# Attention and two mixture layers in one kernel: whole-unit loads of queries, keys and values, and the first weight pair in three tiles of 256 columns

## The chip, the core and the metric

The kernel runs on one core of one Trainium2 chip. The metric is the device time of one execution in microseconds (us), as a median over runs. The engines are named as the profile names them: PE (TensorE matmul) and PEld (its weight loads), DVE (VectorE), ACT (ScalarE), POOL (GpSimd) and SP (SyncE, which issues all DMAs here).

## What is computed

The reference chains three stages; the input sizes stand in the comments.

```
# q, k, v: (2, 8, 768, 64); mem_k, mem_v: (2, 8, 8, 64)
for c in range(24):                       # chunks of 32 queries
    k_full = concat([mem_k, k[:, :, c*32-16 : c*32+32+8]])      # v_full alike
    scores = q_c @ k_full^T / sqrt(64);  a = softmax(scores)
    out[:, :, chunk c] = a @ v_full
x = out as (1536, 512)                    # 2 x 768 tokens, 8 heads x 64
for e in range(4):                        # p: rows of domain_probs, normalised
    y += p[:, e:e+1] * (relu(x @ w1[e]) @ w2[e])                # 512 -> 1024 -> 512
h = y @ w_in;  g = max(h, 0) + alpha * min(h, 0)                # 512 -> 2048
return g @ w_out                                                # 2048 -> 512
```

## The kernel before

**Matmuls.** All large products run in two-part float32r: each operand is split into a high part (`xh`, `wh`) and a low part (`xl`, `wl`), and three matmuls (high by high, high by low, low by high) make one product. The activations are stored transposed: 512 features as four blocks of 128 partitions, the 1,536 tokens as two halves of `NCOL` = 768 columns. The first matmul of every layer (`gemm1`) is a Strassen-like scheme of seven products named a, b, c, d on the PSUM banks they use: 7 x 6 = 42 matmuls a tile. The second (`gemm2`) has 48 matmuls a tile, into `y`. A "pair" `p` is a block of 2 x 128 hidden features; there are 16 pairs of the first layer (`NP1`) and 8 of the second. A "tile" is a pair and a range of columns: `FIRST` lists the ranges for pair 0, all other pairs have two tiles of 384 columns. From pair 1 on the order is gemm1 of the next tile, then gemm2 of this one. For pair 0 all tiles but the last run gemm1 and gemm2 one after the other, which the code calls `tight`.

**Attention.** A unit `u` (0 to 11) is 128 queries of all eight heads. Its work in PE's order is: scores (`two`, 32 matmul instructions, which the trace shows as 64), four transposes (`t`), values (`x`, shown as 32), four transposes back (`xt`). Between them DVE takes the maximum (`mx`) and subtracts it (`pe`), ACT takes the exponential, DVE divides (`dn`, `rd`, `xs`), and ACT, DVE and POOL turn the result into `acc`, `xh` and `xl`, the operands of gemm1, with the sums and differences that the scheme needs (`st`). An even and an odd unit make 128 columns of both halves; c = u // 2 numbers them.

**Order.** `att_cycle` runs the units before the first tile, one a cycle, with some dummy matmuls (`keep`) in each. When enough units are through (`att["five"]`, checked per tile as `c0 + n` over 128), the tile begins, and the remaining units are started by `att_poll` between its matmuls, one each `PACE` of a planned clock `now`. Instructions of each engine stay in the order in which the code emits them; DMAs that are issued through `nc.sync` instead of `sync` (`load`, `load_pb`) may be placed earlier by the scheduler. SP issues its DMAs one by one, and a DMA that waits holds up all behind it.

**Weights.** `prep_w1` and `prep_w2` load a pair's weights (`raw`), form the sums (`s`), and split them (`wh`, `wl`) on ACT and POOL. `gate` normalises the probabilities, `load_pb` spreads them over the partitions, and `convert` reads the second layer's weights, which are 64-bit (`fr`).

**Loads of attention.** Queries and keys of a unit come as two halves (four heads each) of 128 x 624 numbers, into `RING` = 8 buffers. Values come in four DMAs of 64 x 520 numbers, into `RING_V` = 5 half-unit buffers that are cleared once at the start. `load_next_half` and `load_v` issue the later loads from inside `unit`; a load waits until PE has read its buffer's former content.

Of the kernel before, what the change touches and what calls it, by code (L numbers as in the profile page):

```python
# [10 lines left out]
F32 = mybir.dt.float32  # L11
F32R = mybir.dt.float32r
# [6 lines left out]
B, H, S, D = 2, 8, 768, 64  # L19
# [3 lines left out]
NW = BLK // WIN  # L23
# [5 lines left out]
NU = B * NBLK  # L29
NT, DM = B * S, H * D  # L30
E, F1, F2 = 4, 1024, 2048
P = 128
KD = DM // P
HH = H // 2
HP = HH // 2
VW = 2 * HP * NW * (D + 1)
# [30 lines left out]
def tile_kernel(ctx: ExitStack, tc: tile.TileContext, qk, v, wa, wq, dpt, alpha, out):  # L67
# [125 lines left out]
    def mm(*a, n, took=None, **kw):  # L193
        pe_.matmul(*a, **kw)
        now[0] += took or 0.013 + n / 2.4e3


    qk_t = [bp.tile([P, QW + KW], F32, tag="gg" + "BA"[i // 4], bufs=4, name=f"qk{i}") for i in range(RING)]
    v_t = [bp.tile([P, V_ROOM], F32, name=f"v{i}", **tag)[:, :VW].rearrange("p (e z w d) -> p e z w d", e=2, z=HP, w=NW)
           for i, tag in enumerate((dict(tag="w2", bufs=4), dict(tag="w2", bufs=4), dict(tag="fr"), *2 * [dict(tag="v", bufs=2)]))]  # L200
    for vt in v_t:
        for e in range(2):
            (pool, dve)[e].memset(vt[:, e], 0.0)
# [2 lines left out]
    xs = xs.rearrange("p (z e d) -> p z e d", e=2, d=D)  # L206
    pe = pe.rearrange("p (z k e) -> p z k e", e=2, k=KEYS)

    def v_of(hu):
        return v_t[hu % RING_V]  # L210

    def qk_of(hu):
        return qk_t[hu % RING if hu < 2 * RING else hu % (RING // 2)]

    def load_half(hu):
        sync.dma_start(qk_of(hu), qk[hu // 2, :, hu % 2])

    def load_next_half(hu):
        if hu < RING:
            load_half(hu + RING)  # L220
        elif hu < RING + RING // 2:
            load_half(hu + RING)
        elif hu >= 2 * RING and hu + RING // 2 < 2 * NU:
            load_half(hu + RING // 2)

    v_next = [0]

    def load_v(hu):
        assert hu == v_next[0]
        v_next[0] += 1  # L230
        if hu >= 2 * NU:
            return
        for e in range(2):
            sync.dma_start(v_of(hu)[e::2, e].rearrange("p z w d -> p (z w d)"), v[hu // 2, e, :, hu % 2])

    def unit(u):

# [4 lines left out]
        s_ps = two[:, :, :2 * HP * KEYS].rearrange("p e (z k) -> p e z k", k=KEYS)  # L242
        now[0] += T_SW
        for half in range(2):
            qk_ = qk_of(2 * u + half)
            qv = qk_[:, :QW].rearrange("p (z q) -> p z q", q=BLK)
            kv = qk_[:, QW:].rearrange("p (z k) -> p z k", k=SPAN)
            for z in range(HP):
                for w in range(NW):
                    for e in range(2):  # L250
                        rows = slice(e * D, (e + 1) * D)
                        mm(s_ps[win[w], e, HP * half + z], qv[rows, z, win[w]], kv[rows, z, w * STEP:w * STEP + KEYS],
                           n=KEYS, took=T_S, start=True, stop=True)
            load_next_half(2 * u + half)
        mx = cp.tile([P, 2, 2 * HP], F32, tag="mx", bufs=2, name=f"mx{u}")
        dve.tensor_reduce(out=mx, in_=s_ps, axis=AX.X, op=ALU.max)
        dve.tensor_tensor(
# [15 lines left out]
        for z in range(2 * HP):  # L273
            half, i = divmod(z, HP)
            if z in CUT:
                n = CUT[z]
                parts.append((z, n, bank(f"x{u}_{z}")[:, :2 * n * (D + 1)].rearrange("p (z e d) -> p z e d", e=2, d=D + 1)))
            z0, _, x_ps = parts[-1]
            for w in range(NW):
                mm(x_ps[win[w], z - z0], pt[:, z, win[w]], v_of(2 * u + half)[:, :, i, w], n=2 * (D + 1), took=T_X,  # L280
                   start=True, stop=True)
            if i == HP - 1:
                load_v(2 * u + half + RING_V)
        dn = cp.tile([P, 2 * HP, 2, 1], F32, tag="dn", bufs=2, name=f"dn{u}")
        for z, n, x_ps in parts:
            dve.tensor_scalar_add(dn[:, z:z + n], x_ps[:, :, :, D:D + 1], 1e-9)
# [219 lines left out]
    def prep_w2(p):  # L506

        e, dt = pace(p in QUICK and p < NP1, p)
        if p in (NP1, NP1 + 1):
            dt = DT_NEAR  # L510
        yield pause(0.0, lambda: p < 2 or p - 2 in used2)
        if p == 1:
            yield pause(0.0, lambda: att["done"] == NU and (1, 1) in raws)
        if p:
            yield pause(max(0.0, landed[p, 1] - now[0]))
        if p == 0:
            yield pause(0.0, lambda: (0, 1) in raws and landed[0, 1] <= now[0] + 1.0)
        raw = raws[p, 1]
        h = bp.tile([P, 4, 256], F32R, tag="w2", bufs=4, name=f"wh2_{p}")
        l = bp.tile([P, 4, 256], F32R, tag="w2", bufs=4, name=f"wl2_{p}")  # L520
        for z in (0, 2):
            act.copy(h[:, z:z + 2], raw[:, z:z + 2])
            yield pause(1.5 * dt)
            e.tensor_tensor(
                out=l[:, z:z + 2], in0=raw[:, z:z + 2], in1=h[:, z:z + 2].bitcast(F32), op=ALU.subtract
            )
            if z == 2:
                w2[p] = (h, l)
                raws.pop((p, 1))
            yield pause(1.5 * dt)  # L530
        if p == NP1:
            load_raw(p + 2, 0)
        elif 0 < p < NP - 1:
            load_raw(p + 1, 1)
# [95 lines left out]
    def load_pb(e, c0, n, ab=(0, 1)):  # L630
        assert gated
        if (e, c0, n) not in pb_t:
            pb_t[e, c0, n] = bp.tile([P, 2, 384], F32, tag="pb", bufs=2, name=f"pb{e}_{c0}")
        sl = slice(ab[0], ab[-1] + 1)
        nc.sync.dma_start(pb_t[e, c0, n][:, sl, :n], p_dram[e, sl, c0:c0 + n].partition_broadcast(P))
# [20 lines left out]
    def gemm1(p, c0, n, parity, last):  # L656
# [29 lines left out]
        def gelu(blk, src):  # L686

            i, ab = divmod(blk, 2)

            lag_poll(lambda: len(glist) < 2 or glist[-2][1] in glist[-2][0])  # L690
            glist.append((gs, blk))
            if p >= NP1 and i == 0:
                if ab == 0:
                    g2 = bp.tile([P, 2, 384], F32, tag="pb", bufs=2, name=f"g2_{nm}")
                    gs["g2"] = g2
                g = gs["g2"][:, ab, :n]
            else:
                g = bp.tile([P, 384], F32, tag="g", bufs=4, name=f"g{blk}_{nm}")[:, :n]
            gg = bp.tile([P, 2, 384], F32R, tag="gg" + "AB"[parity], bufs=4, name=f"gg{blk}_{nm}")
            gh, gl = gg[:, 0, :n], gg[:, 1, :n]  # L700

            def high():
                act.copy(gh, g)
                pool.tensor_tensor(out=gl, in0=g, in1=gh.bitcast(F32), op=ALU.subtract)
                gs[blk] = (gh, gl)

            def whole():
                dve.scalar_tensor_tensor(out=g, in0=src, scalar=0.0, in1=g,
                                         op0=ALU.max, op1=ALU.add)
                later(0.8, high)  # L710

            if p < NP1:
                pb = pb_t[2 * p * P // F1, c0, n]
                dve.scalar_tensor_tensor(out=g, in0=src, scalar=0.0, in1=pb[:, ab, :n],
                                         op0=ALU.max, op1=ALU.mult)
                later(0.7, high)
            else:
                fi = 2 * (p - NP1) + i

                def negative():  # L720
                    act.activation(g, src, AF.Relu, scale=-1.0)
                    act.mul(g, g, nalpha[:, fi:fi + 1])
                    later(1.4, whole)

                later(0.0, negative)
# [141 lines left out]
        order += [(1, k), (2, k - 1)]  # L867
    order += [(2, len(tiles) - 1)]

    for kind, hu in (*[(load_half, i) for i in range(4)], (load_v, 0), (load_v, 1), (load_half, 4), (load_half, 5),  # L870
                     (load_v, 2), (load_v, 3), (load_half, 6), (load_half, 7), (load_v, 4)):
        kind(hu)
    stream("w", weights())
    streams["w"][0] = PREP0
    acts = {}
    begun = [
        *[(x, lambda: load_raw(0, 0, 4)) for x in (1, 1)],
        (2, lambda: sync.dma_start(praw, dpt.rearrange("e (p i) -> p e i", i=NI))),
        *[(x, lambda: load_raw(0, 0, 4)) for x in (2, 2)],
        (3, lambda: stream("g", gate())),  # L880
        (4, lambda: sync.dma_start(nalpha, alpha)),
        *[(x, lambda ab=ab: load_pb(0, *FIRST[0], (ab,))) for ab, x in enumerate((7, 7))],
        *[(x, lambda: load_raw(0, 1, 2)) for x in (8, 8)],
        (9, lambda: load_pb(0, *FIRST[1], (0,))),
        *[(x, lambda: load_raw(1, 0, 4)) for x in (9, 10, 10, 11)],
        (11, lambda: load_pb(0, *FIRST[1], (1,))),
        *[(x, lambda: load_raw(1, 1, 2)) for x in (12, 12)],
    ]

    def begin():  # L890
# [3 lines left out]
    for i, (what, k, *other) in enumerate(order):  # L894
# [3 lines left out]
        if what == 1:  # L898
# [18 lines left out]
                prep_force(f"x{c0}", lambda: f"x{c0}" not in streams)  # L917
            began.append(k)
            change[0] = kc - 1 <= k < kc + 8
            acts[k] = gemm1(p, c0, n, k % 2, k == final[p])  # L920
        else:
            change[0] = change[0] and k < kc + 6
            if other:
# [3 lines left out]
            if p == NP1 - 2:  # L927
                stream(f"x{c0}", transition(c0, n))

FIRST = [(0, 384), (384, 384)]  # L930
USE = (A11, S2, S1, A12, S3, S4, A22)
SLOTS = 10
WIDE = (NP1 - 1, NP1 + 1)
# [5 lines left out]
CUT = {0: 3, 3: 1}  # L939
FAST = (2, 5)  # L940
LIVE = 4
PACE = 3.8
PACE0 = 3.9
X_STEP = (0.8, 0.8, 0.0, 0.8, 0.8, 0.8)
PREP0 = 11.0

DT = 1.1
DT_0 = 0.78
# [4 lines left out]
DT_X = (1.1, 0.88)  # L953
X_WAIT = (0.0, 7.5)
DT_NEAR = 0.8
RING = 8
V_ROOM = 1152
RING_V = 5
WARM = 18
PAD = 16  # L960

# [73 lines left out]
```

## Time and profile before

| | |
|---|---|
| median of 3 runs | 819.87 us (819.07 to 821.52) |
| profiled execution | 818.88 us, of which the span of the trace is 817.1 us |
| PE busy | 799.2 us (98% of the span) |
| DVE, POOL, ACT busy | 582.5, 563.8, 330.8 us |
| DMA moved | 71.69 MB, of it 16.05 MB in the first 60 us |

PE's busy time is modelled from pipelined matmuls, so 98% says only that PE seldom stands still in what the trace can see; the time of a stretch follows from the starts of its matmuls. Shares are averages over two very different stages: attention, in the first 70 us, and the weight pairs after it.

### The profile page before, as it was taken

The page shows a single profiled execution, that of the slowest core. Times are in us where ns is not written, and L with a number is a line of the kernel's source. Part 1 is how long each engine was busy: PE and PEld are TensorE (multiplying, and loading weights), DVE is VectorE, ACT ScalarE, POOL GpSimd, SP SyncE. Part 2 cuts the span into 40 slices and gives each one's busy share as a digit, 9 for nine tenths or more (in the row PEclk, how much of TensorE's full clock was granted, in tenths as well). Part 3 has the DMA queues.
Part 4 walks back from the last instruction along what each step waited for, and adds up shares of the span by engine and source line. Part 5 has one row for each costly group of instructions (what it writes and reads, how often), then busy time and mean ns, then how long its engine had stood idle before and what let it go on. Part 6 is the DMA issues. An engine that isn't in the chain of part 4 may idle for free.

```text
span 817.1 us, 14814 instructions
## 1 busy us (share of the span) xinstructions
PE 799.2 (98%) x5623; PEld 785.3 (96%) x5623; DVE 582.5 (71%) x1116; ACT 330.8 (40%) x718; POOL 563.8 (69%) x587
## 2 busy tenths in 40 slices
PE   8789999999999999999999999999999999999998
PEld 6578999999999999999999999999899999999998
DVE  4687478777867768867777768587954877756555
ACT  3566523224133223232332323155572665456441
POOL 2777777777877877967887872293954987866611
PEclk9999999999999999999999999999999999999999
DMA  8882121331331431322432312001002142211004
GB/s 286 256 257 69 52 91 39 128 117 54 110 107 42 134 108 57 116 69 74 136 96 85 111 36 72 9 26 53 26 27 91 45 124 82 73 41 52 1 1 155
DMA packets 30503, 71.69 MB, mean 88 GB/s; under 512 B 4704, under 2 KB 9952, under 8 KB 30432
## 3 DMA queue, kind: packets, MB, share of 16 engines
q1 hardware_dynamic: 30432, 70.75, 26.5%
q8 instruction: 44, 0.72, 0.4%
q14 instruction: 27, 0.22, 0.1%
HBM read 59.18 MB, written 11.56 MB: 87 GB/s over the span
## 4 chain that ended last, share of the span: by engine, by line
PE 91%; DVE 3%; ACT 2%; POOL 2%; DMA 1%; issue 1%; DVEq 0%; ACTq 0%; POOLq 0%
PE y L61 48%; PE a L61 12%; PE c L61 11%; PE d L61 11%; PE b L61 6%; POOL gg L61 1%; PE two L61 1%; DMA qk<-in_qk 1%; DVE pe L61 1%; DVE mx L61 1%; PE x L61 1%; PE wps0.0_84 L61 0%; ACT pe L61 0%; DMA raw<-in_wa 0%; PE t L61 0%
## 5 line engine op out<-in xcount | busy, mean ns | idle before, releaser
L61 PE MATMUL y<-gg,wh 128*128 128x384 f32 x1540 | 397.6, 334 | 0.7 <-POOL gg L61 0.6
L61 POOL TENSOR_TENSOR gg<-g,gg 128x384 fp32r<-128x384 f32 x192 | 202.5, 1066 | 118.6 <-ACT gg L61 115.2
L61 PEld LDWEIGHTS y<-gg,wh 128*128 128x128 f32 x1540 | 278.2, 188 | 2.0 <-POOL gg L61 1.2
L61 PE MATMUL y<-gg,wl 128*128 128x384 f32 (+1 forms) x770 | 257.1, 334 | 0.0
L61 DVE TENSOR_TENSOR acc<-y,acc 128x384 f32<-128x384 f32 x321 | 172.1, 550 | 60.9 <-PE y L61 59.3
L61 ACT CAST gg<-g 128x384 fp32r<-128x384 f32 x192 | 97.6, 512 | 152.5 <-DVE g L61 152.3
L61 POOL TENSOR_TENSOR wl<-raw,wh 128x256 fp32r<-128x256 f32 (+1 forms) x112 | 114.3, 1030 | 50.1 <-ACT wh L61 36.2
L61 PEld LDWEIGHTS y<-gg,wl 128*128 128x128 f32 x770 | 144.5, 188 | 0.0
L61 ACT COPY u<-a 128x384 f32<-128x384 f32 x48 | 23.1, 481 | 195.2 <-PE a L61 195.2
L61 POOL TENSOR_TENSOR wl<-s,wh 128x256 fp32r<-128x256 f32 x88 | 68.2, 782 | 7.6 <-ACT wh L61 7.2
L61 DVE TENSOR_TENSOR u<-b,u 128x384 f32<-128x384 f32 x48 | 26.7, 557 | 61.2 <-PE b L61 57.6
L61 PE MATMUL d<-xh,wl 128*128 128x384 f32 x184 | 61.6, 335 | 0.0
L61 PE MATMUL d<-xh,wh 128*128 128x384 f32 x184 | 61.6, 335 | 0.0
L61 PE MATMUL d<-xl,wh 128*128 128x384 f32 x184 | 61.6, 335 | 0.0
L61 PE MATMUL a<-xh,wh 128*128 128x384 f32 x184 | 61.6, 335 | 0.0
L61 PE MATMUL a<-xl,wh 128*128 128x384 f32 x184 | 61.5, 334 | 0.0
L61 PE MATMUL a<-xh,wl 128*128 128x384 f32 x184 | 61.5, 334 | 0.0
L61 ACT CAST wh<-raw 128x256 fp32r<-128x256 f32 (+1 forms) x116 | 54.5, 492 | 15.4 <-PE y L61 14.8
L61 POOL TENSOR_TENSOR fl<-fl,fm 128x512 f32<-128x512 f32 x32 | 41.4, 1292 | 27.4 <-DVE fm L61 18.5
L61 PE MATMUL c<-xh,wh 128*128 128x384 f32 x176 | 59.2, 336 | 0.3 <-DVE b L61 0.3
L61 PE MATMUL c<-xh,wl 128*128 128x384 f32 x176 | 59.0, 335 | 0.0
L61 PE MATMUL c<-xl,wh 128*128 128x384 f32 x176 | 58.9, 335 | 0.0
(117 smaller groups left out, 1357.3 us busy)
## 6 DMA issues: line engine op xcount, KB each, us to landing
fr<-in_wq SPq DMA_DIRECT2D x32, 512.0 KB, 3.8
raw<-in_wa SPq DMA_DIRECT2D x28, 512.0 KB, 3.8
w2s<-fl SPq DMA_DIRECT2D x32, 256.0 KB, 2.4
raw<-w2s SPq DMA_DIRECT2D x16, 512.0 KB, 3.6
qk<-in_qk SPq DMA_DIRECT2D x24, 312.0 KB, 4.5
v<-in_v SPq DMA_DIRECT2D x48, 130.0 KB, 4.0
outT<-acc SPq DMA_DIRECT2D x15, 192.0 KB, 1.8
pb<-p_dram SPq DMA_DIRECT2D x6, 384.0 KB, 3.5
```

The costliest lines, as they stand in the source:

```text
L61: return self.tc.keep_in_program_order(f(*a, **kw))
```

## The change

Queries and keys of a unit are loaded by one DMA of 128 x 1,248 numbers (the first unit's still by two), values by two DMAs of 64 x 1,040 numbers. The rings become 4 units of queries and keys (2 from unit 8 on) and 2 units of values. The high and low parts of `w2` share a tile, and so do the two `gg` blocks of one hidden block. Pair 0 is cut into three tiles of 256 columns: the first needs c = 0 and 1, that is units 0 to 3, where it needed units 0 to 5. `PACE` goes from 3.8 to 4.8 and `PREP0` from 11.0 to 8.0; the list `begun`, which ties loads to the count of units started, is shorter.

```diff
-    qk_t = [bp.tile([P, QW + KW], F32, tag="gg" + "BA"[i // 4], bufs=4, name=f"qk{i}") for i in range(RING)]
-    v_t = [bp.tile([P, V_ROOM], F32, name=f"v{i}", **tag)[:, :VW].rearrange("p (e z w d) -> p e z w d", e=2, z=HP, w=NW)
-           for i, tag in enumerate((dict(tag="w2", bufs=4), dict(tag="w2", bufs=4), dict(tag="fr"), *2 * [dict(tag="v", bufs=2)]))]
+    qk_t = [bp.tile([P, 2, QW + KW], F32, tag="gg" + "AB"[i // 2], bufs=2, name=f"qk{i}") for i in range(RING)]
+    v_t = [bp.tile([P, V_ROOM], F32, name=f"v{i}", **tag)[:, :2 * VW].rearrange("p (e h z w d) -> p e h z w d", e=2, h=2, z=HP, w=NW)
+           for i, tag in enumerate((dict(tag="w2", bufs=2), dict(tag="v", bufs=1)))]
...
+    def load_qk(u, half=slice(0, 2)):
+        if u < NU:
+            sync.dma_start(qk_of(u)[:, half].rearrange("p h x -> p (h x)"), qk[u, :, half].rearrange("p h x -> p (h x)"))
+
+    def load_v(u):
+        if u < NU:
+            for e in range(2):
+                sync.dma_start(v_of(u)[e::2, e].rearrange("p h z w d -> p (h z w d)"), v[u, e].rearrange("p h x -> p (h x)"))
...
-            if i == HP - 1:
-                load_v(2 * u + half + RING_V)
+        load_v(u + RING_V)
+        if u < RING:
+            load_qk(u + RING)
...
-    for kind, hu in (*[(load_half, i) for i in range(4)], (load_v, 0), (load_v, 1), (load_half, 4), (load_half, 5),
-                     (load_v, 2), (load_v, 3), (load_half, 6), (load_half, 7), (load_v, 4)):
-        kind(hu)
+    for half in range(2):
+        load_qk(0, slice(half, half + 1))
+    load_v(0)
+    load_qk(1)
+    load_v(1)
+    load_qk(2)
+    load_raw(0, 0)
+    load_qk(3)
+    sync.dma_start(praw, dpt.rearrange("e (p i) -> p e i", i=NI))
...
-FIRST = [(0, 384), (384, 384)]
+FIRST = [(0, 256), (256, 256), (512, 256)]
...
-PACE = 3.8
+PACE = 4.8
...
-PREP0 = 11.0
+PREP0 = 8.0
...
-RING = 8
-V_ROOM = 1152
-RING_V = 5
+RING = 4
+V_ROOM = 2304
+RING_V = 2
```

The order of instructions shows three places. The first is SP's queue at the start of the program. Before (numbers after a name are buffers; each `v` row is two DMAs):

```order
L61 DMA qk0_109<-in_qk 128x624
L61 DMA qk1_110<-in_qk 128x624
L61 DMA qk2_111<-in_qk 128x624
L61 DMA qk3_112<-in_qk 128x624
L61 DMA v0_117<-in_v 64x520 x2
L61 DMA v1_118<-in_v 64x520 x2
L61 DMA qk4_113<-in_qk 128x624
L61 DMA qk5_114<-in_qk 128x624
L61 DMA v2_119<-in_v 64x520 x2
L61 DMA v3_120<-in_v 64x520 x2
L61 DMA qk6_115<-in_qk 128x624
L61 DMA qk7_116<-in_qk 128x624
```

The same queue of the changed kernel from its first DMA on:

```order
L61 DMA qk0_109<-in_qk 128x624 x2
L547 DMA fr0_1827<-in_wq 128x1024
L61 DMA v0_113<-in_v 64x1040 x2
L61 DMA qk1_110<-in_qk 128x1248
L61 DMA v1_114<-in_v 64x1040 x2
L61 DMA qk2_111<-in_qk 128x1248
L61 DMA raw0_0_131<-in_wa 128x1024
L61 DMA qk3_112<-in_qk 128x1248
L61 DMA praw_104<-in_dpt 128x4x12
L61 DMA v0_113<-in_v 64x1040 x2
L61 DMA qk0_109<-in_qk 128x1248
```

The first pair's weights (`raw0_0`) now come whole and between the units, the first block of the second layer's weights (`fr0`) has moved to the front of the queue, and the values of unit 2 (the second `v0_113`) stand behind the keys of unit 3.

The second place is PE where the first tile begins. Before, from the dummy matmuls of the eighth cycle on:

```order
L61 MATMUL keep7_863<-xh_105 128x384 x3
L61 MATMUL t7_867<-ident_73,pe_134 128x128 x4
L61 MATMUL xt6_873<-ident_73,xs_133 128x128 x4
L61 MATMUL x7_0_881<-v4_121,pt_132 32x130 x8
L61 MATMUL x7_0_881<-v0_117,pt_132 32x130 x4
L61 MATMUL x7_3_896<-v0_117,pt_132 32x130 x4
L61 MATMUL two_72<-qk0_109 32x64 x16
L61 MATMUL two_72<-qk1_110 32x64 x16
L61 MATMUL a0_0_880<-xh_105,wh1_0_0_556 128x384
```

Changed:

```order
L61 MATMUL keep6_720<-xh_105 128x384 x3
L61 MATMUL t6_724<-ident_73,pe_121 128x128 x4
L61 MATMUL xt5_730<-ident_73,xs_120 128x128 x4
L61 MATMUL x6_0_755<-v0_113,pt_119 32x130 x12
L61 MATMUL x6_3_768<-v0_113,pt_119 32x130 x4
L61 MATMUL two_72<-qk3_112 32x64 x32
L61 MATMUL a0_0_750<-xh_105,wh1_0_0_451 128x256
```

The first tile's first matmul (`a0_0`) stands one cycle earlier: behind the scores of unit 7 where it stood behind those of unit 8.

The third place is DVE near the end of the first tile. Before, the sums of pair 1's weights (`s_1`) stand behind or just ahead of the last unit's division:

```order
L61 SCALAR_TENSOR_TENSOR g2_0_0_1281<-c0_0_1086,pb0_0_755 128x384
L61 TENSOR_TENSOR s_1_1310<-raw0_1_950 128x256
L61 TENSOR_SCALAR dn11_1334<-x11_0_1316 128x6
L61 TENSOR_SCALAR dn11_1334<-x11_3_1329 128x2
L61 RECIPROCAL rd11_1337<-dn11_1334 128x8
```

Changed:

```order
L61 SCALAR_TENSOR_TENSOR g2_0_0_1054<-c0_0_873,pb0_0_624 128x256
L61 TENSOR_TENSOR s_1_1095<-raw0_1_938 128x256
L61 TENSOR_REDUCE mx10_1130<-two_72 128x8
L61 TENSOR_TENSOR pe_121<-two_72,mx10_1130 128x2x256
L61 TENSOR_SCALAR dn9_1154<-x9_0_1134 128x6
```

They now come while units 9 to 11 are still to be done on DVE.

## Rows read from the trace of the kernel before

**Rows 1.** Chain that ended last, 74 to 100 us: start, us, what

```profile
90.98 8.32 PE y L61 x48
```

**Rows 2.** Timeline of PE, 68 to 93 us: start, us, instruction, xcount

```profile
70.79 0.60 PE L61 MATMUL xt<-ident,xs 128*128 128x128 f32 x4
...
76.26 0.33 PE L61 MATMUL a<-xh,wh 128*128 128x384 f32 x1
```

**Rows 3.** Windows: stretch, length, busy us (xcount) per engine, PE clock, DMA, GB/s

```profile
47.74:70.79 23.05, 22.62 (x419) 19.22 (x414) 20.43 (x50) 14.31 (x29) 15.70 (x15) 1.00 0.70 221
```

**Rows 4.** Timeline of PE, 4.5 to 48 us, with [idle before <-releaser]

```profile
4.92 1.18 PE L61 MATMUL two<-qk 64*32 64x64 f32 x64
...
17.21 0.62 PE L61 MATMUL two<-qk 64*32 64x64 f32 x36
19.45 0.45 PE L61 MATMUL two<-qk 64*32 64x64 f32 x28 [1.62 <-issue]
...
21.91 0.65 PE L61 MATMUL x<-v,pt 128*32 128x130 f32 x16 [1.43 <-DMA v<-in_v]
...
27.11 0.32 PE L61 MATMUL two<-qk 64*32 64x64 f32 x9 [2.02 <-issue]
...
35.66 0.86 PE L61 MATMUL two<-qk 64*32 64x64 f32 x64
...
39.79 0.86 PE L61 MATMUL two<-qk 64*32 64x64 f32 x64
...
44.60 0.66 PE L61 MATMUL t<-ident,pe 128*128 128x128 f32 x4 [2.21 <-ACT pe L61]
45.09 0.60 PE L61 MATMUL xt<-ident,xs 128*128 128x128 f32 x4
45.93 1.09 PE L61 MATMUL x<-v,pt 128*32 128x130 f32 x32 [0.24 <-ACT pt L61]
46.95 0.86 PE L61 MATMUL two<-qk 64*32 64x64 f32 x64
47.74 0.44 PE L61 MATMUL a<-xh,wh 128*128 128x384 f32 x1
```

**Rows 5.** Windows of attention's first units, columns as in rows 3

```profile
10.00:20.00 10.00, 7.40 (x222) 5.69 (x217) 5.25 (x16) 3.70 (x7) 1.28 (x1) 1.00 0.95 311
20.00:30.00 10.00, 5.68 (x142) 4.07 (x134) 5.67 (x16) 2.87 (x6) 5.52 (x10) 1.00 0.92 278
```

**Rows 6.** DMA issues, 0 to 60 us: count, KB each, median us to landing

```profile
qk<-in_qk SPq DMA_DIRECT2D x24, 312.0 KB, 4.5
v<-in_v SPq DMA_DIRECT2D x48, 130.0 KB, 4.0
```

**Rows 7.** DMA queues, 17.0 to 17.2 us: packets, MB, share of 16 engines

```profile
q8 instruction: 1, 0.02, 27.5%
```

**Rows 8.** Timeline of PE at the kernel's end

```profile
812.72 0.28 PE L61 MATMUL y<-gg,wl 128*128 128x192 f32 x1
...
813.06 0.28 PE L61 MATMUL y<-gg,wl 128*128 128x192 f32 x1
```

**Rows 9.** Timeline of DVE, 42 to 46 us

```profile
42.48 0.68 DVE L61 TENSOR_REDUCE mx<-two 128x8 f32<-128x512 f32 x1
...
43.80 0.22 DVE L61 TENSOR_SCALAR dn<-x 128x6 f32<-128x6 f32 x2
...
45.09 1.06 DVE L61 TENSOR_TENSOR xl<-acc,xh 128x512 fp32r<-128x512 f32 x1
```

**Rows 10.** DVE groups, 47.74 to 70.79 us: xcount, busy us, mean ns, idle

```profile
L61 DVE TENSOR_TENSOR s<-raw 128x256 f32<-128x256 f32 x2 | 2.4, 1180 | 0.0
...
L61 DVE TENSOR_TENSOR st<-xt,st 128x256 f32<-128x256 f32 x2 | 0.8, 414 | 0.0
...
L61 DVE TENSOR_TENSOR u<-b,u 128x384 f32<-128x384 f32 x1 | 0.6, 558 | 0.0
```

More of the change, by code (lines that the diff above doesn't have):

```diff
@@ L207, in tile_kernel, with v_of, qk_of @@
     pe = pe.rearrange("p (z k e) -> p z k e", e=2, k=KEYS)
[L209 to L234, printed above, removed]
+    def v_of(u):
+        return v_t[u % RING_V]
+    def qk_of(u):
+        return qk_t[u % RING if u < 2 * RING else RING // 2 + u % (RING // 2)]
+    def load_qk(u, half=slice(0, 2)):
[5 more added lines that the diff above has]
+                sync.dma_start(v_of(u)[e::2, e].rearrange("p h z w d -> p (h z w d)"), v[u, e].rearrange("p h x -> p (h x)"))
     def unit(u):
@@ L244, in unit @@
         for half in range(2):
-            qk_ = qk_of(2 * u + half)
+            qk_ = qk_of(u)[:, half]
             qv = qk_[:, :QW].rearrange("p (z q) -> p z q", q=BLK)
@@ L253, in unit @@
                            n=KEYS, took=T_S, start=True, stop=True)
-            load_next_half(2 * u + half)
+        if u + RING // 2 >= 2 * RING:
+            load_qk(u + RING // 2)
         mx = cp.tile([P, 2, 2 * HP], F32, tag="mx", bufs=2, name=f"mx{u}")
@@ L279, in unit @@
             for w in range(NW):
-                mm(x_ps[win[w], z - z0], pt[:, z, win[w]], v_of(2 * u + half)[:, :, i, w], n=2 * (D + 1), took=T_X,
+                mm(x_ps[win[w], z - z0], pt[:, z, win[w]], v_of(u)[:, :, half, i, w], n=2 * (D + 1), took=T_X,
                    start=True, stop=True)
-            if i == HP - 1:
-                load_v(2 * u + half + RING_V)
+        load_v(u + RING_V)
+        if u < RING:
+            load_qk(u + RING)
         dn = cp.tile([P, 2 * HP, 2, 1], F32, tag="dn", bufs=2, name=f"dn{u}")
@@ L518, in prep_w2 @@
         raw = raws[p, 1]
-        h = bp.tile([P, 4, 256], F32R, tag="w2", bufs=4, name=f"wh2_{p}")
-        l = bp.tile([P, 4, 256], F32R, tag="w2", bufs=4, name=f"wl2_{p}")
+        hl = bp.tile([P, 2, 4, 256], F32R, tag="w2", bufs=2, name=f"w2_{p}")
+        h, l = hl[:, 0], hl[:, 1]
         for z in (0, 2):
@@ L698, in gelu @@
                 g = bp.tile([P, 384], F32, tag="g", bufs=4, name=f"g{blk}_{nm}")[:, :n]
-            gg = bp.tile([P, 2, 384], F32R, tag="gg" + "AB"[parity], bufs=4, name=f"gg{blk}_{nm}")
+            if ("gg", i) not in gs:
+                gs["gg", i] = bp.tile([P, 2, 2, 384], F32R, tag="gg" + "AB"[parity], bufs=2, name=f"gg{i}_{nm}")
+            gg = gs["gg", i][:, ab]
             gh, gl = gg[:, 0, :n], gg[:, 1, :n]
@@ L876, in tile_kernel @@
     begun = [
-        *[(x, lambda: load_raw(0, 0, 4)) for x in (1, 1)],
-        (2, lambda: sync.dma_start(praw, dpt.rearrange("e (p i) -> p e i", i=NI))),
-        *[(x, lambda: load_raw(0, 0, 4)) for x in (2, 2)],
         (3, lambda: stream("g", gate())),
[L881 to L887, printed above, removed]
+        (3, lambda: sync.dma_start(nalpha, alpha)),
+        (4, lambda: load_raw(0, 1)),
+        *[(6, lambda ab=ab: load_pb(0, *FIRST[0], (ab,))) for ab in range(2)],
+        (8, lambda: load_pb(0, *FIRST[1])),
+        (9, lambda: load_raw(1, 0)),
+        (12, lambda: load_raw(1, 1)),
     ]
@@ L919, in tile_kernel @@
             change[0] = kc - 1 <= k < kc + 8
-            acts[k] = gemm1(p, c0, n, k % 2, k == final[p])
+            acts[k] = gemm1(p, c0, n, 0 if k < k0 else (k - k0 + 1) % 2, k == final[p])
         else:
```

## The prediction

> **What bounds the kernel now.** I read the shares first (PE 98%), then the chain that ended last. From 69 us on it is PE alone: the 48 matmuls of one second half take 8.32 us [rows 1], 0.1733 us for a matmul of 384 columns, so the 90 of a tile take 15.6 us. The first tile of pair 0 hands over at 76.26 [rows 2]; with 15.6 us more, pair 0's 180 matmuls are paid off at 91.9. (Half of the second tile's stand behind pair 1's first ones; that changes no sum.) Behind 91.9 the change moves nothing: same tiles, same order on PE, so the time moves by as much as 91.9 does.
>
> Ahead of it there are two stages, split where the first tile begins at 47.74 [rows 4].
>
> Stage one is attention alone. The reader should look at the starts of the scores: units 0 to 3 start at 4.92 to 17.21, a cycle of 4.10 us. Unit 6 would then start at 29.5, and starts at 35.66: 6.1 us are lost. Three idle times make up 5.1 of them: 1.62 and 2.02 behind "issue" in the middle of the scores, and 1.43 for the values of unit 2 [rows 4]. In these stretches the DMA engines are 95% and 92% busy at 311 and 278 GB/s [rows 5]. A packet of the queue that brings instructions begins at 17.0 to 17.2 [rows 7], and PE runs dry at 17.8 and goes on at 19.45. I read "issue" there as PE waiting for its own instructions, behind the data.
>
> Stage two, 47.74 to 91.9, is 44.1 us: 31.2 for 180 matmuls and 12.9 for the rest. By start to start, a unit's scores take 0.79, values 1.02, transposes 0.49 and 0.60 [rows 4]; three, four, four and five of them are 11.4 us, which leaves 1.5 of stalls. DVE is 20.43 of 23.05 us busy up to the last unit's transposes [rows 3].
>
> **What the change does, step by step.**
>
> *Begin of the first tile.* It needs two units fewer and begins one cycle earlier in PE's order, behind unit 7's scores. That last cycle was 7.95 us (39.79 to 47.74), of which 2.21 was a wait on exponentials where the other cycles have about 0.5 [rows 4]; DVE was then at `acc` of the units 4 and 5, which now fall behind the begin. I take 7.95 - 1.7 = 6.2 from unit 6's scores to the first `a`.
>
> *Data in time?* A unit is 0.64 MB of queries and keys (two of 312 KB) and 0.27 MB of values (two of 130 KB) [rows 6]; `raw` and `fr` are 0.52 each. At 0.31 MB/us [rows 5] the new queue, up to the values of unit 2, is 4.4 MB, 14 us; begun at about 1.8 it ends at 16, and unit 2's values are wanted at 18.2 (19.83 less the 1.62). The wait of 1.43 goes. `fr0` ahead of unit 1 brings that unit in at 8.5, wanted at 8.9: 0 to 0.3; I take 0.3.
>
> *Instructions.* PE's stream to this point is the same, so it runs dry at the same places. By my count of SP's queue 1.5 MB lie ahead of the first refill where 1.1 did: 1.62 x 1.5 / 1.1 = 2.2, with some room 2.4 (bounds 0 and, if the whole depth doubles, 5.5). For the second, at 24 us, the queue has run down to some 0.25 MB, since the first pair's weights came early: 0 (bound 2.02).
>
> So unit 6 starts at 29.5 + 0.3 + 2.4 = 32.2 and the first `a` at **38.4** instead of 47.7. Bounds: 35.7 with no loss, 40.4 with the second refill, 44 with the deep queue.
>
> *One unit more in stage two.* Each of the four kinds of work once more: **+2.9**. This is most of what was gained ahead: a cycle's PE work is moved, only its idle time is saved.
>
> *Narrower matmuls.* 270 of 256 columns for 180 of 384: the same columns. No such matmul is in the trace. Three of 192 columns take 0.34 us, 0.113 each [rows 8]: with that for a floor 270 take 30.5 (-0.7); on the straight line between 0.113 and 0.1733 they take 0.133, 36.0 (+4.8). At the granted clock of 1.00, that is 2.4 GHz, 384 columns are 0.160, which leaves 0.013 a matmul; 256 are 0.107, with the same 0.013 it is 0.120, 32.4 us: **+1.2**. I take it since 0.120 lies above the floor. The Trainium skill, "TensorE: Matmul & The Clock Gate", section "Back-to-back issue gap", gives columns over 2.4 plus 2.5 ns for a warm matmul by itself, and says that streams with weight loads deviate: by that estimate 0.109, 29.5 us, a gain of 1.7. The row of 192 columns does not agree: 0.113 against 0.083.
>
> *DVE in stage two.* It gets work earlier in the tile. A maximum and a subtraction are 1.32, a division 1.29, an `xl` 1.06 [rows 9], a sum `s` 1.18 and a 256-column operation 0.41 against 0.56 [rows 10]. Up to the last division, against before: one maximum and subtraction (+1.3), a division and a half (+1.9), one `xl` (+1.1), two or more of the `s` that now come ahead of the last units (+2.5), nine narrower operations of the scheme (-1.3): 20.4 + 5.5 = 25.9. With the 2.6 that DVE stood idle in the same stretch of before [rows 3] it is 28.5. PE's own work to the same point (five values, five transposes forward, five back, four scores, 13.7; 92 matmuls, 11.0; the division, 1.3) is 26.0. So 2.5 of stalls, 0 if DVE idles less. Then the second tile, still `tight`: DVE has nine operations of 0.41 and about 3 us of the last unit's, 6.9 us for 42 matmuls of 5.0; the second half's first matmuls need only the first results, so 1.7 of it shows. Together 4.2 where there were 1.5: **+2.7**, bounds 0 and +5.
>
> *Nothing for:* `gg` and `w2` in shared tiles (pair 0's tiles are `tight`, and a buffer is written 24 matmuls, 2.9 us, after its last reader; uncovered, at most one such wait, 2.9); third ranges for `acc`, covered by 5.8 us of second-half matmuls; pair 1's weights, which are wanted over 40 us later than they are loaded; the keys behind `pb`, about a 4 us landing [rows 6] on SP, covered by the one-cycle lead of the ring of four.
>
> **Sum.** 38.4 + 44.1 + 2.9 + 1.2 + 2.7 = 89.3, against 91.9: 2.6 us less. Of its own time, 818.88, that makes 816.3. The profiled execution is 0.99 under the median, from which it would be 817.3; I give 816.8, between. What a measurement tells from no change here is 0.3%, 2.5 us, so the forecast lies right at that bound.
>
> **Rivals.**
>
> *B: hidden refills, DVE dense.* If instructions come ahead of the data and DVE fills its idle time, the tile begins at 35.7 and stage two has no added stall: 35.7 + 44.1 + 2.9 + 1.2 = 83.9, 8 us less, about 811.5. For it: the larger transfers end earlier, and DVE's 2.6 us of idle time are waits for PE, which shrink as it gets behind. Against it: the DMA engines are no less busy at 17 us. The Trainium skill, "Runtime: NRT & Kernel Launch", section "Instruction fetch mechanics", is on its side: blocks of 16 KiB are fetched while the one before runs, at a cost that is mostly hidden. The idle times of 1.62 and 2.02 do not bear it out. Chance 0.20.
>
> *C: swallowed.* Both refills stay (3.6 together instead of 2.4: begin at 39.6) and DVE's idle time repeats in the second tile too (+4): 39.6 + 44.1 + 2.9 + 1.2 + 4 = 91.8, no change, 819.8. For it: the DMA engines moved 278 GB/s in the second stretch also [rows 5]. Chance 0.27.
>
> *D: slower.* The refill packets queue behind transfers of twice the size. With the sum's other terms at 50.9 it decides at a begin of 41.0; at 44, the bound above, pair 0 ends at 94.9, 3 us later: 822.8. For it: larger transfers stand in every queue ahead of the packet. Against: the bytes are the same, and the queue runs down earlier. Chance 0.15.
>
> *A, the forecast:* 0.38, its own range 814.5 to 819.
>
> **How the numbers follow.** B and 0.27 of A are faster by over 0.3%, 0.47. C but for 0.05 and 0.11 of A are within, 0.33. D and that 0.05 are slower, 0.20. From 811.5 to 822.3 leaves out half of B's lower side and part of D.
>
> **What would show it.** Right: the first `a` near 38.4; no wait for values at unit 2; one "issue" wait of about 2.4 in `two`, not two; 0.120 between narrow matmuls; DVE over 90% busy from there to the last division; PE's waits there near 4; pair 1's tiles at 15.6 us. Wrong: an "issue" wait above 5, narrow matmuls at 0.133 (then 3.6 us slower than summed), or any new wait behind 100 us, which would mean that the loads or the planner moved work that I took for unchanged.

## The result and the profile after

The changed kernel takes 827.72 us (median of 4 runs), the kernel before beside it 819.54: a ratio of 1.0092, interval 1.0073 to 1.0112. It is slower by 0.9%; I had forecast 816.8, in a range from 811.5 to 822.3. Its profiled execution took 827.92 us, span 826.1.

I read the same two stages. The timeline of PE answers to [rows 4] and [rows 2] (start, us, instruction, count, idle time before and its releaser):

```profile
4.42 0.86 PE L61 MATMUL two<-qk 64*32 64x64 f32 x64
...
10.61 1.16 PE L61 MATMUL two<-qk 64*32 64x64 f32 x64 [2.41 <-DMA qk<-in_qk]
11.70 1.96 PE L61 MATMUL x<-v,pt 128*32 128x130 f32 x32
...
16.21 1.09 PE L61 MATMUL x<-v,pt 128*32 128x130 f32 x32
...
23.66 0.79 PE L61 MATMUL two<-qk 64*32 64x64 f32 x57
25.75 0.31 PE L61 MATMUL two<-qk 64*32 64x64 f32 x7 [1.30 <-issue]
...
31.25 0.85 PE L61 MATMUL x<-v,pt 128*32 128x130 f32 x19 [0.48 <-issue]
...
33.83 0.86 PE L61 MATMUL two<-qk 64*32 64x64 f32 x64
...
38.36 1.01 PE L61 MATMUL keep<-xh 128*128 128x384 f32 x2 [2.27 <-issue]
...
42.98 0.39 PE L61 MATMUL a<-xh,wh 128*128 128x256 f32 x1
43.20 0.28 PE L61 MATMUL a<-xl,wh 128*128 128x256 f32 x1
...
44.16 0.28 PE L61 MATMUL b<-xh,wh 128*128 128x256 f32 x1
...
90.25 0.28 PE L61 MATMUL a<-xh,wh 128*128 128x256 f32 x1
```

The first tile begins at 42.98, 4.8 us earlier than before and 4.6 later than forecast. The last of the three tiles begins at 90.25; with 90 matmuls of 0.12 more, pair 0 is paid off at 101.0, where it was 91.9. Those 9.1 us are the whole loss of this trace (the span grew by 9.0; the medians differ by 8.2). Stage two, from 42.98 on, is 58.1 us; it was 44.1, and the forecast 50.9.

Windows of three stretches of low clock and of the first tile, columns as in [rows 3]:

```profile
10.60:14.40 3.80, 3.79 (x99) 3.12 (x100) 2.15 (x6) 0.63 (x1) 0.00 (x0) 0.55 0.99 369
38.36:42.20 3.84, 3.84 (x45) 3.19 (x45) 0.58 (x2) 1.57 (x4) 1.50 (x3) 0.61 0.49 102
62.00:66.00 4.00, 4.00 (x104) 3.33 (x103) 1.42 (x4) 1.79 (x3) 3.62 (x3) 0.59 0.01 4
42.98:74.69 31.71, 26.48 (x520) 23.00 (x515) 21.36 (x58) 17.95 (x42) 18.55 (x19) 0.95 0.58 206
```

The granted clock fell to little over half behind idle times of 2.41 and 2.27 us and behind a series of short ones from 57 to 61. The first tile's stretch is the one to compare with the forecast of DVE: 21.36 us busy of 31.71 (of 31.0 up to the last unit's transposes back, at 74.01), not 25.9 of 28.5. DVE was not full. PE waited all the same; PE's waits from 42.98 to 101 (in total, times, longest):

```profile
PE y L61 <- POOL gg L61: 1.7, 2, 1.4
PE xt L61 <- DVE xs L61: 1.5, 1, 1.5
PE c L61 <- DVE b L61: 1.2, 2, 0.6
PE t L61 <- ACT pe L61: 1.1, 2, 0.9
PE y L61 <- DVE dn L61: 0.7, 1, 0.7
PE y L61 <- ACT gg L61: 0.6, 1, 0.6
PE y L61 <- DVE xs L61: 0.4, 1, 0.4
PE x L61 <- ACT pt L61: 0.2, 1, 0.2
```

The same view of the kernel before, from 47 to 100 us, has a single line:

```profile
PE y L61 <- POOL gg L61: 0.2, 1, 0.2
```

Where the second half of the first tile begins in the changed kernel, its waits stand in a row in the timeline, three matmuls apart:

```profile
56.82 0.52 PE L61 MATMUL y<-gg,w 128*128 128x256 f32 x3
58.08 0.59 PE L61 MATMUL y<-gg,w 128*128 128x256 f32 x3 [0.75 <-DVE dn L61]
59.05 0.59 PE L61 MATMUL y<-gg,w 128*128 128x256 f32 x3 [0.38 <-DVE xs L61]
60.26 0.50 PE L61 MATMUL y<-gg,w 128*128 128x256 f32 x2 [0.62 <-ACT gg L61]
61.06 0.63 PE L61 MATMUL y<-gg,w 128*128 128x256 f32 x3 [0.30 <-POOL gg L61]
```

### The profile page after: what moved, and what is told of

The parts are those of the page before. It is cut to its first block, busy times and chain, and to the rows that moved or that the text cites. A ratio compares the mean times of both kernels' runs of the same rounds, so it can differ in the third digit from the quotient of the medians.

```text
span 826.1 us, 14877 instructions
## 1 busy us (share of the span) xinstructions
PE 804.1 (97%) x5710; PEld 790.2 (96%) x5710; DVE 580.4 (70%) x1122; ACT 333.1 (40%) x731; POOL 563.4 (68%) x588
## 4 chain that ended last, share of the span: by engine, by line
PE 90%; DVE 4%; POOL 2%; ACT 2%; issue 2%; DMA 1%; SPq 0%; DVEq 0%; ACTq 0%; POOLq 0%
PE y L61 47%; PE a L61 11%; PE c L61 11%; PE d L61 11%; PE b L61 6%; POOL gg L61 1%; PE two L61 1%; PE x L61 1%; DMA qk<-in_qk 1%; PE t L61 1%; DVE pe L61 1%; DVE mx L61 1%; PE xt L61 1%; POOL xl L61 0%; ACT xh L61 0%
## 5 line engine op out<-in xcount | busy, mean ns | idle before, releaser
L61 PE MATMUL y<-gg,w 128*128 128x384 f32 (+1 forms) x2358 | 410.6, 331 | 3.7 <-POOL gg L61 1.9
L61 PEld LDWEIGHTS y<-gg,w 128*128 128x128 f32 x2358 | 402.1, 188 | 5.6 <-POOL gg L61 2.9
L61 POOL TENSOR_TENSOR gg<-g,gg 128x384 fp32r<-128x384 f32 (+1 forms) x196 | 202.6, 1044 | 117.1 <-ACT gg L61 115.7
L61 ACT CAST gg<-g 128x384 fp32r<-128x384 f32 (+1 forms) x196 | 98.4, 505 | 156.3 <-DVE g L61 156.2
L61 PE MATMUL a<-xh,wh 128*128 128x384 f32 (+1 forms) x188 | 62.4, 332 | 0.0
L61 PE MATMUL a<-xh,wl 128*128 128x384 f32 (+1 forms) x188 | 62.4, 332 | 0.0
L61 PE MATMUL d<-xh,wh 128*128 128x384 f32 (+1 forms) x188 | 62.3, 331 | 0.0
L61 PE MATMUL d<-xh,wl 128*128 128x384 f32 (+1 forms) x188 | 62.2, 331 | 0.0
L61 PE MATMUL d<-xl,wh 128*128 128x384 f32 (+1 forms) x188 | 62.2, 331 | 0.0
L61 PE MATMUL a<-xl,wh 128*128 128x384 f32 (+1 forms) x188 | 62.2, 331 | 0.0
```

The costliest lines, as they stand in the source:

```text
L61: return self.tc.keep_in_program_order(f(*a, **kw))
```

## The experiments

A trace is one execution. The waits for data and instructions in stage one differ from run to run (the kernel before took 818.3 to 824.6 us beside these runs), so times are given as ratios to the kernel before with their intervals, and the trace's stages beside them. "End" is the end of pair 0, counted as above; where pair 1's first matmuls come between, from their start and the 48 matmuls of 0.12 still owed. Stage two too varies: the changed kernel, e4 and e10 run the same tiles in the same order and have 58.1 to 59.0. So a difference of about 1 us between two traces is not shown to be the edit's.

| kernel | first `a` | stage two | end | ratio, interval |
|---|---|---|---|---|
| before | 47.7 | 44.1 | 91.9 | |
| changed | 43.0 | 58.1 | 101.0 | 1.0092 (1.0073 to 1.0112) |
| e1_loads | 49.7 | 45.6 | 95.3 | 1.0011 (0.9997 to 1.0025) |
| e2_tiles | 45.0 | 58.9 | 103.9 | 1.0135 (1.0111 to 1.0159) |
| e3_fr_late | 41.4 | 56.5 | 97.9 | 1.0073 (1.0050 to 1.0096) |
| e4_warm36 | 41.8 | 58.9 | 100.7 | 1.0099 (1.0066 to 1.0131) |
| e5_keys_first | 42.6 | 56.3 | 98.8 | 1.0059 (1.0031 to 1.0086) |
| e6_two_tiles | 49.3 | 45.2 | 94.5 | 1.0004 (0.9986 to 1.0022) |
| e7_pace38 | 42.0 | 55.1 | 97.1 | 1.0031 (1.0015 to 1.0047) |
| e8_untight | 42.5 | 54.6 | 97.1 | 1.0032 (1.0018 to 1.0047) |
| e9_late_begin | 47.8 | 49.7 | 97.5 | 1.0049 (1.0033 to 1.0064) |
| e10_no_values | 39.3 | 59.0 | 98.3 | one run |
| e11_untight_pace | 42.8 | 53.9 | 96.8 | 1.0054 (1.0039 to 1.0069) |
| e12_ring6 | 48.0 | 44.2 | 92.2 | 0.9990 (0.9979 to 1.0001) |
| e13_xl_pool | 42.0 | 54.8 | 96.8 | 1.0058 (1.0039 to 1.0076) |
| e14_late_untight | 48.9 | 46.7 | 95.6 | 1.0029 (1.0015 to 1.0044) |

In every one of these traces the span less "end" is between 724.9 and 725.8 us: nothing behind pair 0 changes, whatever is done ahead of it.

**Loads alone, tiles alone.** e1 is the changed kernel with

```diff
-FIRST = [(0, 256), (256, 256), (512, 256)]
+FIRST = [(0, 384), (384, 384)]
...
-PACE = 4.8
+PACE = 3.8
...
-PREP0 = 8.0
+PREP0 = 11.0
```

> The new loads (whole units, merged tiles, fr0 ahead of unit 1) with the old two tiles of 384 columns, old PACE and PREP0. Theory 1 (loads and tiles each do their own harm): unit 1 waits about 2.4 us for its keys as in the changed kernel, the third refill costs about 2.3 us, the first tile begins near 47 and the rest is as before, 44 us: 819 to 821 us. Theory 2 (the loads do all the harm): stage two stays near 58 us, 827 us or more. Theory 3 (the tiles do all of it): the begin is earlier than before, 812 to 817 us.

e2 is the kernel before with those three lines the other way round, and two lines that go with the tiles (`gg` buffers alternate from pair 1 on, the first `pb` comes one unit earlier).

> The old loads with the three tiles of 256 columns, PACE 4.8 and PREP0 8.0. Theory 1: the first tile begins near 42, stage two takes about 57 us instead of 44, end of pair 0 near 99: 826 to 828 us. Theory 2 (loads do all the harm): stage two near 51 us, 819 to 821 us. Theory 3 (tiles do all of it): as the changed kernel, 827 to 829 us.

e1 cannot be told from before. e2 took 831.7 us, above all three of its ranges. So the tiles, with their PACE and PREP0, do the harm, and they do it in stage two, as theory 1 had it: 58.9 with them and 45.6 without. The new loads don't gain by themselves; in e1 unit 1 waits 2.46 us for its keys too.

**What the front of the queue costs.** e3 keeps the first load of the second layer's weights at its place in the code:

```diff
-            nc.sync.dma_start(raw.rearrange("p f w -> p (f w)"), ...)
+            (nc.sync if k else sync).dma_start(raw.rearrange("p f w -> p (f w)"), ...)
```

> The changed kernel with the first load of the second layer's weights kept at its place in the code instead of ahead of unit 1. Theory 1: no wait for the keys of unit 1 and no low clock behind it, unit 2's scores start near 12.5 instead of 15.4, and the end moves by as much, 3 us: near 824.7 us. Rival: the transfers of whole units come late by themselves, the wait moves by under 0.7 us and the time stays within 826.5 to 828.5 us; or the 3 us are lost again at the next refill, same time.

The wait for the keys fell from 2.41 to 1.51 and the low clock behind it went; the end came 3.1 us earlier in the trace. Half of that is stage two, where e3 had no low clock; the median went from 827.7 to 826.3 only, with intervals that overlap, nearer to the rival than to the theory. e5 also puts the keys of unit 1 ahead of the values of unit 0:

```diff
-    load_v(0)
     load_qk(1)
+    load_v(0)
```

> The three tiles, with the second layer's first load late and the keys of unit 1 ahead of the values of unit 0. Theory (the data's order cost the start of attention): unit 1 waits under 0.5 us for its keys (1.5 with the load late alone), the first tile begins near 39.8 and the end moves by as much, to about 824.5 us. Rival (the instruction refills take back what the data gives): begin near 41.4 as with the load late alone, 826 us.

The wait for keys is gone. But in the timeline of e5, another stands in the scores of unit 2:

```profile
8.14 0.86 PE L61 MATMUL two<-qk 64*32 64x64 f32 x64
...
12.27 0.41 PE L61 MATMUL two<-qk 64*32 64x64 f32 x18
14.87 0.95 PE L61 MATMUL two<-qk 64*32 64x64 f32 x46 [2.19 <-issue]
```

The rival was right: a refill took back what the data gave, and the median is 826.0.

e6 is e5 with e1's lines.

> The same order of loads with the old two tiles of 384 columns, old PACE and PREP0. If the tiles are what harms and the loads are good once the order is mended: begin near 46, stage two 44 to 46 us, end of pair 0 near 91, 817.5 to 820 us. If whole units lose to half units by themselves: begin at 48 or later, 821 us or more.

No change (1.0004), begin 49.3: whole units in the better order are no faster than half units.

**Are the waits behind "issue" instruction blocks?** e4 has twice as many warm-up matmuls of half the width:

```diff
-WARM = 18
+WARM = 36
...
-pe_.matmul(wps[:, :2 * P]..., warm, warm.unsqueeze(1).to_broadcast([P, 2, P]),
+pe_.matmul(wps[:, :P], warm, warm,
```

> The changed kernel with 36 warm-up matmuls of 128 columns for 18 of 256: the same columns, 36 more PE instructions (with the weight loads) ahead of all else. If the idle times behind issue are PE running out of its instructions, they keep their place in the count of instructions and so stand 18 matmuls of the program earlier: the one in the scores of unit 4 (57 of 64 records) near record 21, the one in the dummy matmuls behind unit 6's values inside the values. If they belong to what PE does there, they stay. Time within 1 us of the changed kernel's either way.

The timeline of e4, the scores of units 4 and 5:

```profile
24.37 0.64 PE L61 MATMUL two<-qk 64*32 64x64 f32 x39
26.19 0.43 PE L61 MATMUL two<-qk 64*32 64x64 f32 x25 [1.17 <-issue]
...
29.94 0.81 PE L61 MATMUL two<-qk 64*32 64x64 f32 x59
31.93 0.31 PE L61 MATMUL two<-qk 64*32 64x64 f32 x5 [1.19 <-issue]
```

Unit 4's wait went from record 57 to record 39, and the next one from record 13 of the values (record 77 of that cycle) to 59: both by 18. I had expected record 21, having counted a warm-up matmul as two records; it is one. The third wait, due inside unit 6's values, did not come. The waits that come keep their place in the count of instructions. In the changed kernel they lie 127 records apart (from record 57 of unit 4: 7 of scores, 32 of values, 3 dummies, 8 transposes, 64 of scores, 13 of values), 254 instructions with the weight loads.

e10 leaves out the loads of values from unit 2 on:

```diff
     def load_v(u):
-        if u < NU:
+        if u < 2:
```

> The changed kernel without the loads of values from unit 2 on: 2.6 MB less in the first 50 us (the values of units 0 and 1 are used again and again). If the waits behind issue are instruction blocks that stand behind data at full DMA engines: those from unit 2 on shrink, to under 0.5 us each beyond the first 20 us, the first tile begins at 38 to 39.5 instead of 43. If they are something else of PE's: they stay at 1.3, 0.5 and 2.3 us, begin within 1 us of 43.

The timeline of PE and one window of e10:

```profile
20.94 0.44 PE L61 MATMUL two<-qk 64*32 64x64 f32 x27 [0.58 <-issue]
24.69 0.86 PE L61 MATMUL two<-qk 64*32 64x64 f32 x64
28.81 0.86 PE L61 MATMUL two<-qk 64*32 64x64 f32 x64
32.98 0.86 PE L61 MATMUL two<-qk 64*32 64x64 f32 x64
...
39.28 0.39 PE L61 MATMUL a<-xh,wh 128*128 128x256 f32 x1
```

```profile
20.00:38.00 18.00, 15.05 (x444) 11.72 (x424) 13.47 (x38) 11.90 (x27) 12.79 (x19) 1.00 0.39 125
```

With the DMA engines 39% busy from 20 to 38 us (75% in the changed kernel), no wait is left behind 20.94; the cycle is 4.1 us again, and the first `a` is 6.3 us behind unit 6's scores, as the forecast's 6.2 had it. So the waits hang on the data's traffic, and with their place in the count (e4) I read them as waits for blocks of instructions. How a block is held up is less plain. In the changed kernel the queues at 36.0 to 36.5 us (packets, MB, share of 16 engines) show

```profile
q8 instruction: 1, 0.02, 12.0%
```

a packet of the instruction queue that begins as the wait begins (36.09 to 38.36). The DMA engines were 95% busy from 34 to 35 us, 67% from 35 to 36, and 4% from 37 to 38, and PE went on only at 38.36: most of this wait fell into a time without data traffic. Whether the packet had stood behind the data or was asked for late, the trace does not tell. The end of e10, however, came only 2.8 us earlier than the changed kernel's: stage two grew to 59.0, with a wait of 2.6 us at the first transposes back.

e12 is the kernel before with a shallower start, six half-unit buffers in turn (`hu % 6` for the units 0 to 5, then `hu % 4`):

```diff
-        return qk_t[hu % RING if hu < 2 * RING else hu % (RING // 2)]
+        return qk_t[hu % 6 if hu < 12 else hu % 4]
...
-        (load_v, 2), (load_v, 3), (load_half, 6), (load_half, 7), (load_v, 4)):
+        (load_v, 2), (load_v, 3), (load_v, 4)):
```

> The kernel before with six half-unit buffers of queries and keys in turn instead of eight for the units 0 to 5, so that 0.64 MB less stands in the DMA queues at the start. If the depth of the queues is what PE's instruction blocks wait behind: the two waits of 1.62 and 2.02 us shrink by a third or more and the first tile begins 1 us or more earlier: 817.5 to 819 us. If only the bytes count: no change, 819.5 to 820.5 us; if the keys come late instead: waits of two for keys, 821 us or more.

The first wait fell from 1.62 to 0.89, the second stayed 2.02, a third of 1.72 came up behind them; the time did not change by what can be measured. In this trace less depth at the start moved the waits and did not remove them.

**Why stage two is long.** e9 is e5 with a begin after six units, as before:

```diff
-                while att["five"] < -(-(c0 + n) // BLK):
+                while att["five"] < max(3, -(-(c0 + n) // BLK)):
```

> As e5_keys_first, but the first of the three tiles begins only when six units are through, as in the kernel before. Theory 1 (a narrow tight tile is the cause: too few matmuls between the links of a unit's chain, whatever unit it is): begin near 47, stage two 53 us or more, end of pair 0 at 100 or later, 828 us or more. Theory 2 (the early begin is the cause, with one unit more in the tile): stage two near 47 us, end of pair 0 near 94, 821 to 823 us.

Neither: 49.7. Against e5, the early begin brings the first tile 5.2 us forward and makes stage two 6.6 longer, 2.9 of it the unit's own work as forecast; the time is the same (1.0049 and 1.0059). Against before, stage two is 5.6 longer; against e6, which has the same loads and differs in the tiles, PACE and PREP0, 4.5. PE's waits in e9 from 47.78 to 100:

```profile
PE c L61 <- DVE b L61: 1.2, 2, 0.6
PE y L61 <- DVE dn L61: 0.7, 1, 0.7
PE y L61 <- ACT gg L61: 0.6, 1, 0.6
PE y L61 <- DVE xs L61: 0.6, 1, 0.6
PE y L61 <- POOL gg L61: 0.3, 1, 0.3
PE x L61 <- ACT pt L61: 0.2, 1, 0.2
```

e14 gives e9 the order of the later pairs, first half of the next tile ahead of second half of this one:

```diff
-    for k in range(k0 - 1):
-        order += [(1, k), (2, k)]
-    order += [(1, k0 - 1)]
-    for k in range(k0, kc + 1):
+    order += [(1, 0)]
+    for k in range(1, kc + 1):
...
-        tight = p == 0 and c0 + n < NCOL
+        tight = False
```

The `gg` buffers then alternate from the first tile on.

> As e9_late_begin (begin with six units), with the halves of pair 0 in the order of the later pairs. There stage two took 49.7 us, of which about 3.4 were waits at y, c and t in the first two tiles. If the tight order is what leaves the narrow tile's waits uncovered: waits of y gone, stage two 46.5 to 47.5 us, 821.5 to 822.5 us. If narrow tiles wait whatever the order, because one unit's chain is longer than the matmuls between its links: stage two 49 or more, time as e9_late_begin within 1 us.

Its waits from 48.95 to 100:

```profile
PE x L61 <- ACT pt L61: 0.6, 1, 0.6
PE c L61 <- DVE b L61: 0.6, 1, 0.6
PE c L61 <- DVE dn L61: 0.5, 1, 0.5
```

All waits of `y` are gone and stage two is 46.7, in the forecast span (the median, 822.7, is just above its own). So it is the tight order that left these waits uncovered. In the traces stage two is 3.0 of the 5.6 us shorter: PE's waits went from 3.6 to 1.7, and 0.35 is low clock that only e9 had at its first matmuls (its first ten took 1.63 us, those of e14 1.28). The medians say less: 1.0049 to 1.0029, some 1.6 us, with intervals that overlap a little.

e8 is the same order on e5, with the early begin; e7 is e5 with PACE 3.8; e11 both, on e3's loads.

> As e5_keys_first, but pair 0's halves in the order of the later pairs: first half of the next tile, then second half of this one, so that 42 matmuls lie between a tile's last product and its first y. Theory 1: PE's waits in y for gg, dn, xs (about 3.5 us together) go, the low clock behind them too; stage two 52 to 53 us where e5_keys_first has 56 to 57, time 820 to 821 us. Rival (DVE's amount of work sets stage two, not where PE meets it): the waits turn up at t, xt and c instead, stage two stays above 55, time within 1.5 us of e5_keys_first.

> As e5_keys_first, with PACE 3.8 again: units start closer together between the first tile's matmuls. Theory 1 (the second half of a tight tile stands uncovered behind its first): waits of y stay, stage two 56 us or more, time within 1.5 us of e5_keys_first. Theory 2 (the planner's wider pace makes stage two long): stage two at 53 us or less, 3 us faster than e5_keys_first.

> Three tiles with the second layer's first load late, the halves in the order of the later pairs, and PACE 3.8 together. Each of the two by itself brought stage two from 56.3 to 54.6 and 55.1 us. If they mend different waits: stage two near 53.5, about 822 us. If they mend the same: 54.5 and 823.5 us or more. Still slower than the kernel before.

In e8 the waits of `y` went, but new ones stand at `c` for `b` (2.5, were 1.2) and at `b` for `xl` (1.0): 54.6, between theory and rival. PACE brought 1.2 us in the trace, between its two theories too. Together they came to 53.9, near 53.5, but the time to 1.0054, not better than either; by time they do not add up.

e13 takes the step that stood ahead of unit 6's division off DVE:

```diff
-FAST = (2, 5)
+FAST = (5,)
```

> As e5_keys_first, but the low part of the columns of units 4 and 5 is formed by POOL instead of DVE (and in a later step of the planner), so that DVE's division of unit 6 does not stand behind a step that waits for ACT. Theory (the early begin meets ACT and POOL still splitting the first pair's weights and these columns): PE's wait of about 1 us at unit 6's transposes back goes, but POOL's queue grows; stage two 55 to 56 us against 56.3, time within 1.5 us of e5_keys_first. Rival (that one wait starts the others): stage two at 53.5 or less, 3 us faster.

The wait at the transposes back is gone, and stage two is 54.8, 1.5 less, of which the wait was 1.0. It did not start the others, and the time is e5's.

No version here beats the kernel before; e12's interval ends at 1.0001.

## Why the prediction was wrong, point by point

**What bounds and what carries over: right.** Only the end of pair 0 moves the time; some 725 us behind it in 16 traces.

**Stage two, "Together 4.2 where there were 1.5: +2.7": the step that failed most.** I made the stalls out of the amount of DVE's work, 25.9 us in 28.5. DVE was 21.36 us busy in 31.71. The `s` that I priced at 1.18 took 0.62 or 0.42 on average, by form.

Stage two grew by 14.0 us where the sum had 6.8. At the sum's own prices (14.3 us for the units' work, 32.4 for 270 matmuls) 11.4 of its 58.1 us are stalls, not 4.2. PE's waits listed above are 7.4 of them; before the change they were 0.2 of the 1.5 that I called stalls. About 1.4 is low clock: PE was busy 50.6 us in stage two of the changed kernel, but 49.2 in e3 and e5, where nearly the same waits brought no fall of the clock. The rest, some 2.6, I put down to slow first matmuls behind a change of kind; no run measures it by itself.

I looked for a full engine; what cost was a chain: PE's product, DVE, ACT, POOL, PE, with the attention's steps in the same queues, and at a tight tile of 256 columns too few matmuls between its ends. The same tight order cost the kernel before 0.2 us at `y`: its matmuls were half as long again and had one unit fewer among them. Which of the two spared it is not shown. I had given the second tile 1.7 for this and the first none.

The parts, by the traces: in e9, which begins late, 1.2 for the narrower matmuls as forecast, up to 3.0 that went with the tight order (e14), 1.4 not split further. The early begin adds 6.6 (e5 against e9): 2.9 as forecast and 3.7 beyond it. Nearly all of the 3.7 is in three waits of e5, from 42.56 to 98.8:

```profile
PE y L61 <- POOL gg L61: 1.7, 2, 1.4
PE t L61 <- ACT pe L61: 1.1, 2, 0.9
PE xt L61 <- DVE xs L61: 1.0, 1, 1.0
```

In e9 the first is 0.3 and the others are absent. The last is unit 6's division behind an `xl` that waits for ACT, and goes in e13; what makes the first two I have not settled. The changed kernel's remaining 1.8 over e5 is the low clock (1.4) and 0.5 more at the transposes back.

**The begin at 38.4: too early by 4.6.** *Data in time:* `fr0` ahead of unit 1 was to cost 0 to 0.3. The keys were there at 10.6, not 8.5, and the wait was 2.41, since I let the queue run in order: up to 10.6 us the trace shows 3.02 MB moved, not the 2.07 up to these keys, so loads issued behind them had shared the engines. *Instructions:* "2.4, and the second 0". The first did not come; then 1.30, 0.48 and 2.27. I treated the blocks as two events at the places where they had shown; the waits of this trace are 254 instructions apart, and whether one comes at such a place, and how long it is, changes from one trace to the next. Unit 6 started at 33.83 instead of 32.2, and the last cycle took 9.15 instead of 6.2: the 2.27 and the low clock behind it. That clock was in no term of mine: a rival of its own, unseen.

**Right in kind and size:** 0.12 us for 256 columns (43.20 to 44.16, eight matmuls, in the timeline); the wait for unit 2's values gone (16.21); the last cycle of 6.2 (e10); nothing from the merged `gg` and `w2` tiles, since e1 and e6 equal before in time. One unit more at 2.9 was not measured by itself.

**The rivals.** D put the slower outcome on the begin: 44 us, 822.8. The begin was near that, 43.0, but of the 11.7 us by which pair 0 ended later than forecast 7.2 are stage two's: the outcome was D's, for a reason that D did not have. C had the stalls of stage two at about the forecast's size. None had PE waiting beside a DVE with time to spare.

On instruction blocks, the Trainium skill, "Runtime: NRT & Kernel Launch", section "Instruction fetch mechanics", says that blocks of 256 instructions are fetched ahead and mostly hidden. The spacing of 254 agrees; that they are hidden holds in e10 (DMA engines 39% busy from 20 to 38 us), not in the changed kernel (75%).

## What to carry to other kernels

Starting a stage earlier is worth only the idle time it removes: its work moves along, and so do its dependences. Before narrowing a tile, follow one chain from its last product through the other engines to the first matmul that needs it, and count the matmuls that remain between; a share of busy time below 100% on every engine does not say that they suffice. And while DMA queues are full, reckon with waits of PE for its instructions: what an earlier load gains, such a wait may take back, as in e5.

## What the runs showed of the hardware

Idle times of PE behind "issue" keep their place in the count of instructions: 18 matmuls more at the start moved two of them by exactly 18 records, and a third did not come. They lasted 0.5 to 2.3 us in the changed kernel, with the DMA engines 75% busy from 20 to 38 us, and were absent from 21 us on with 39%.

The granted clock fell to a mean of 0.55 to 0.61 in three stretches of about 4 us; within them, from 12 to 14, 38 to 40 and 62 to 64 us, it was 0.50, the lower of its two levels (1.2 and 2.4 GHz). PE had idled 2.41 and 2.27 us ahead of the first two, and several times for 0.3 to 0.8 us ahead of the third. A run of values then took 1.96 us instead of 1.09. Such idle times do not always bring it: the kernel before idled 2.02 and 2.21 us [rows 4] at a clock of 1.00, and e5 and e3 had the same wait at the same instruction:

```profile
37.73 0.78 PE L61 MATMUL keep<-xh 128*128 128x384 f32 x2 [1.72 <-issue]
37.83 0.62 PE L61 MATMUL keep<-xh 128*128 128x384 f32 x2 [1.72 <-issue]
```

In e5 (the first line) the clock from 38 to 40 us was 0.50, in e3 1.00.
